# Moving the stack transfers of an attention-plus-GLU kernel into one unit, and shifting its score ring by 64 bytes

## The chip, the core and the metric

The kernel runs on one core of a Trainium2 chip. A core has TensorE (PE, matmuls; its weight loads are listed as PEld), VectorE (DVE), ScalarE (ACT), GpSimd (POOL) and SyncE (SP), which here issues nearly all DMA transfers. They work on SBUF, a memory of 128 partitions; matmuls write to PSUM. The metric is the device time of one execution in microseconds, the median over several runs; lower is better.

## The reference

The input x has 2048 rows (tokens) of 512 features. Two branches are mixed by a gate:

```
g = sigmoid(sum(x * gate_w))                     # one number per row
a = attention(x): qkv = x @ wqkv, 32 heads of 16 features,
    query i sees keys i-255 .. i (a sliding window of 256),
    softmax(q k^T / 4) v, then @ wo
b = (sigmoid(x @ w_gate) * (x @ w_up)) @ w_down  # 1376 inner features
out = g * a + (1 - g) * b
```

All of it is float32. The kernel keeps that accuracy by splitting a number into a high and a low part and adding three matmuls (high by high, high by low, low by high).

## The kernel before

**Tiles.** The rows are cut into 16 blocks of 128 (NB) and 4 chunks of 512 (NC), the heads into 8 groups of 4 (NG). One *unit* is one block of one head group; 128 units, numbered u, make the attention part, and the loop over u from L839 on writes down the work of all engines in the order in which they run it. A *score matmul* is one of the four per unit that `s_part` makes (L370, queries by keys, to find each row's maximum) or that `st_part` makes (L425, keys by queries, whose exponentials become the softmax weights). `st_part` runs 9 units behind `s_part` (LAG).

**Half-array matmuls.** A score matmul contracts 64 rows, half of TensorE. `s_part` and `st_part` take opposite halves, so one matmul of each goes through side by side. Between them stand the matmuls of the projections (`pj`) and of the GLU branch (`gu`), L282, which are split into two halves of 64 rows in the same manner. In every unit a pair of score matmuls is followed by two or three such pairs. Every 8 units, at u = 17, 25, 33, and so on, stands a burst of `pv` matmuls (L460, weights by values).

**The score ring.** The operands of the score matmuls lie in `ring`, three places of 16 KB per partition, each holding one *stack*: the queries and keys of 8 units (1024 columns), with extra rows for the low parts, for constants and for the row maxima. A stack is made thus: the projection is split into `sh` (high) and `sl` (low), both are stored to DRAM (`stack_scratch<-sh`, `stack_scratch<-sl`, 512 KB each), and they are read back in rows of another order by `stack_load`: one fill of constants (two for the first use of a place), one transfer of 512 KB and four of 256 KB, all into `ring`. The list is put into `sdma` at u = 9 for stack 2, and at u = 18, 26, 34, ... for the stacks 3 to 15. `transfers()` then issues at most SD = 3 of them in each unit (a module constant on L44), in the order in which SP reaches them, and with them what else is due: stores of finished `gu` tiles (`gu_scratch<-sp`), loads of the next GLU weights (`guraw`).

**The maxima.** A group of four units gives a table of row maxima. It is split on VectorE (`max_split`), stored to DRAM (`max_scratch<-nt`, L394, 16 KB) and read back into `ring` by two transfers of 8 KB (`max_load`, L401). The `st_part` matmuls of those rows need it, through the 128-byte pieces that it puts into the ring. From u = 13 on SP issues the store and the load in every fourth unit (13, 17, 21, ...), for the group that began five units earlier. The first two groups have their stores at u = 4 and 8 and their loads at u = 5 and 9, where the load stands behind `transfers()`.

**The issue order.** SP takes its transfers one after another, each with its waits, so a transfer that waits holds up all that stand behind it. All of them share 16 DMA engines.

**Addresses.** SBUF tiles are placed in the order in which they are declared. Before the change `ring` starts at byte 2176 of each partition, which is 128 modulo 256; x (`xh`, `xl`) and all weights of L282 start at 192 modulo 256. In the last part, the down projection (`pd`), `hb` are the stationary operands, at 128 modulo 256, and `ring` holds the moving ones.

Of the kernel before, what the change touches and what calls it, by code (L numbers as in the profile page):

```python
# [7 lines left out]
F32 = mybir.dt.float32  # L8
# [6 lines left out]
P = 128  # L15
# [9 lines left out]
NB = T // P  # L25
# [15 lines left out]
PVLAG = LAG + 4  # L41
WIDE = 2 * 4
NWIDE = NG - 1
SD = 3  # L44
QB = 32
HOLD = 3
GAPS = [3] * 12 + [2] * 3
# [18 lines left out]
def gated_mix_kernel(  # L66
# [40 lines left out]

    cpool = ctx.enter_context(tc.tile_pool(name="cpool", bufs=1))
    ps = ctx.enter_context(tc.tile_pool(name="ps", bufs=1, space=PSUM))
    ring_t = cpool.tile([P, 4, RING * CH2], F32R, name="ring")  # L110
    ring = [ring_t[:, :, r * CH2:(r + 1) * CH2] for r in range(RING)]
    gsum = cpool.tile([P, NB], F32, name="gsum")


    def ring_f(f):
# [28 lines left out]
    with ExitStack() as actx:  # L144
# [197 lines left out]
        def run_dmas(dmas):  # L342
            for dst, src in dmas:
                nc.sync.dma_start(dst, src)
# [494 lines left out]
        for u in range(N):  # L839
# [19 lines left out]
            def transfers():  # L859
# [5 lines left out]
                later.clear()  # L865
                run_dmas(sdma[:SD])
                del sdma[:SD]

# [116 lines left out]
            if u == N - 1:  # L985
                pctx.close()
                lpool = actx.enter_context(tc.tile_pool(name="lpool", bufs=1))
                gates = lpool.tile([P, 4 * NB], F32, name="gates")
                gs, omg = gates[:, 0:NB], gates[:, NB:2 * NB]
                spare = [lpool.tile([P, CH], F32, name=f"spare{k}") for k in range(6)]  # L990
            if u >= N - 2:
# [168 lines left out]
```

## Time and profile before

| | |
|---|---|
| three runs | 724.72, 722.93, 725.45 us; median 724.72 us |
| the profiled execution | 723.27 us |
| its span, first to last instruction | 721.4 us |
| TensorE busy | 713.5 us (99% of the span) |
| VectorE, ScalarE, GpSimd busy | 478.5, 430.4, 165.6 us |
| the 16 DMA engines, mean busy share over the span | 56.2% for SP's queue |
| granted TensorE clock, mean | 1.000 |

The profile gives for each group of instructions its line, engine, operands, count, busy time, mean length and the idle time before it with what ended that. A wait of TensorE can be seen twice: on PE (the matmul) and on PEld (the weight load that runs ahead of it). Matmuls are pipelined, so a matmul's length (0.39 us for 512 columns) is more than the distance from one start to the next on the same rows of the array; that distance is what a matmul costs.

### The profile page before, as it was taken

What the parts mean: (1) busy time and instruction counts of PE and PEld (TensorE: products, weight loads), DVE (VectorE), ACT (ScalarE), POOL (GpSimd) and SP (SyncE); (2) the same over time, 40 slices, a digit from 0 to 9 for tenths busy, and PEclk for the clock granted to TensorE, in tenths of its full rate; (3) what the DMA queues carried; (4) which work ended last, traced back from release to release, by engine and by line L of the source; (5) the groups of instructions that cost most, each with busy time, mean ns of one, the idle gap of its engine ahead of it and who ended that gap; (6) DMA issues with size and microseconds to landing.
All of it is one profiled execution on the core that took longest, in us unless ns stands there. A gap on an engine that the chain in (4) does not pass through costs nothing.

```text
span 721.4 us, 17549 instructions
## 1 busy us (share of the span) xinstructions
PE 713.5 (99%) x6298; PEld 606.1 (84%) x6298; DVE 478.5 (66%) x1455; ACT 430.4 (60%) x890; POOL 165.6 (23%) x254
## 2 busy tenths in 40 slices
PE   9999999999999999999999999999999999999997
PEld 7888889888798798988979889798788888888886
DVE  5369767657676676765667667676837767667481
ACT  6423766667676677766767667675676655435341
POOL 5200423223233233323324223232331000000000
PEclk9999999999999999999999999999999999999999
DMA  8465534646355364554645437465478978778531
GB/s 304 112 201 195 202 123 177 189 137 212 127 195 189 121 211 146 178 165 146 203 149 197 152 99 245 151 219 148 154 216 227 263 201 215 199 169 250 144 65 58
DMA packets 104814, 127.22 MB, mean 176 GB/s; under 512 B 46718, under 2 KB 63614, under 8 KB 104728
## 3 DMA queue, kind: packets, MB, share of 16 engines
q1 hardware_dynamic: 104584, 125.98, 56.2%
q8 instruction: 49, 0.80, 0.5%
q14 instruction: 37, 0.30, 0.1%
q10 hardware_dynamic: 144, 0.13, 0.1%
HBM read 71.80 MB, written 51.13 MB: 170 GB/s over the span
## 4 chain that ended last, share of the span: by engine, by line
PE 98%; DMA 1%; issue 0%; DVE 0%; DVEq 0%
PE gu L282 28%; PE pj L282 12%; PE pv L460 11%; PE s L370 6%; PE st L425 6%; PE tp L598 6%; PE pd L96 5%; PE pd L95 5%; PE pd L94 5%; PE vh L635 3%; PE pa L94 2%; PE pa L95 2%; PE pa L96 2%; PE vps L497 2%; DMA ring<-max_scratch 1%; PE pd L1088 1%
## 5 line engine op out<-in xcount | busy, mean ns | idle before, releaser
L376 DVE CUSTOM_DVE_ANT_0 junk<-s,mask 128x384 f32<-128x384 f32 (+2 forms) x512 | 271.9, 531 | 136.8 <-PE s L370 76.4
L282 PE MATMUL gu<-xh,w 64*128 64x512 f32 x1152 | 273.5, 392 | 0.0
L282 PE MATMUL gu<-xl,w 64*128 64x512 f32 x576 | 185.9, 389 | 0.0
L430 ACT ACTIVATE pbuf<-st 128x384 f32<-128x384 f32 (+2 forms) x288 | 138.3, 490 | 60.7 <-PE st L425 31.3
L425 PE MATMUL st<-ring 64*128 64x384 f32 (+2 forms) x536 | 166.6, 327 | 2.7 <-DMA ring<-max_scratch 2.5
L370 PE MATMUL s<-ring 64*128 64x384 f32 (+2 forms) x536 | 162.9, 322 | 0.0
L282 PEld LDWEIGHTS gu<-xh,w 64*128 64x128 f32 x1152 | 157.0, 185 | 5.3
L430 ACT ACTIVATE V<-st 128x384 f32<-128x384 f32 (+2 forms) x224 | 100.6, 454 | 51.9 <-PE s L370 24.9
L370 PEld LDWEIGHTS s<-ring 64*128 64x128 f32 x536 | 95.2, 184 | 14.1 <-issue 3.0
L436 POOL TENSOR_SCALAR_AFFINE_SELECT pbuf<-pbuf 128x512 f32<-128x512 f32 x72 | 46.8, 651 | 253.2 <-ACT pbuf L430 239.1
L425 PEld LDWEIGHTS st<-ring 64*128 64x128 f32 x536 | 95.9, 184 | 7.7 <-DMA ring<-max_scratch 1.9
L282 PEld LDWEIGHTS gu<-xl,w 64*128 64x128 f32 x576 | 92.0, 185 | 1.6
L282 PE MATMUL pj<-xl,wqh 64*128 64x512 f32 (+1 forms) x228 | 79.9, 389 | 0.0
L282 PE MATMUL pj<-xh,wqh 64*128 64x512 f32 (+1 forms) x228 | 79.8, 389 | 0.0
L282 PE MATMUL pj<-xh,wql 64*128 64x512 f32 (+1 forms) x228 | 69.8, 389 | 0.0
L95 PE MATMUL pd<-ring,hb 128*128 128x512 f32 x160 | 62.3, 390 | 0.0
L94 PE MATMUL pd<-ring,hb 128*128 128x512 f32 x160 | 62.3, 390 | 0.0
L96 PE MATMUL pd<-ring,hb 128*128 128x512 f32 x160 | 62.3, 390 | 0.0
L436 POOL TENSOR_SCALAR_AFFINE_SELECT V<-V 128x512 f32<-128x512 f32 x56 | 35.8, 640 | 111.2 <-ACT V L430 107.1
L90 ACT CAST hb<-V 128x512 fp32r<-128x512 f32 x40 | 24.9, 622 | 58.8 <-DVE V L798 44.2
L460 PE MATMUL pv<-pbuf,V 128*32 128x384 f32 (+2 forms) x848 | 49.5, 382 | 0.0
L442 POOL TENSOR_SCALAR_AFFINE_SELECT pbuf<-pbuf 128x512 f32<-128x512 f32 x70 | 44.9, 641 | 0.0
(131 smaller groups left out, 1243.4 us busy)
## 6 DMA issues: line engine op xcount, KB each, us to landing
gu_scratch<-sp SPq DMA_DIRECT2D x72, 256.0 KB
V<-gu_scratch SPq DMA_DIRECT2D x36, 512.0 KB
ring<-stack_scratch SPq DMA_DIRECT2D x56, 256.0 KB
stack_scratch<-sh SPq DMA_DIRECT2D x14, 512.0 KB
stack_scratch<-sl SPq DMA_DIRECT2D x14, 512.0 KB
ring<-stack_scratch SPq DMA_DIRECT2D x14, 512.0 KB
guraw<-in_wgu_dram SPq DMA_DIRECT2D x18, 256.0 KB
v_scratch<-V SPq DMA_DIRECT2D x4, 1088.0 KB
```

The costliest lines, as they stand in the source:

```text
L94: mm(ps, lh, rh, start=first, stop=False)
L95: mm(ps, lh, rl, start=False, stop=False)
L96: mm(ps, ll, rh, start=False, stop=last)
L282: return mm(pt, (wl if w == 2 else wh)[r, d], (xl if w == 1 else xh)[r, d, c * CH:(c + 1) * CH], start=k == 0 and not second, stop=k == 3 ...
L370: mm(pt[:, (k - k0) * P:(e - k0) * P], lhsT, blk(g, k, hh, 1, e - k), start=k == k0, stop=e == i + 1, skip_group_check=True,)
L376: nc.vector.tensor_tensor_reduce(junk[:, 0:n], pt[:, 0:n], mask[:, 3 * P - n:], scale=1.0, scalar=NEG, op0=ALU.add, op1=ALU.max, accum_out ...
L425: mm(pt[:, (q - j) * P:(e - j) * P], lhsT, blk(g, q, hh, 0, e - q), start=q == j, stop=e == last, skip_group_check=True,)
L430: exps.append(nc.scalar.activation(p_blk(u, hh, 0, n), pt[:, 0:n * P].rearrange("p (b t) -> p b t", t=P), AF.Exp, scale=SCALE,))
L436: nc.gpsimd.affine_select(buf[:, s0], buf[:, s0], pattern=[[0, HG], [1, P]], compare_op=ALU.is_ge, fill=0.0, base=0, channel_multiplier=-1,)
L442: nc.gpsimd.affine_select(old, old, pattern=[[0, HG], [-1, P]], compare_op=ALU.is_gt, fill=0.0, base=0, channel_multiplier=1,)
L460: mm(bank[32 * hh:32 * hh + w, (q - q0) * P:(e - q0) * P], vt[:, v:v + w], p_blk(g * NB + j, hh, q - j, e - q), start=j == j0, stop=j == q ...
L598: return mm(tp[b][:, 0:TW], (xl if w == 1 else xh)[r, d, b * P:(b + 1) * P], tw[d][int(w == 2)][r, 0:TW], start=k == 0 and not second, sto ...
```

## The change

Two things are changed.

First, SD goes from 3 to 7, so that all transfers of a stack are issued in the unit in which the list is made: u = 9 for stack 2 and u = 18, 26, ... for the others, each one unit behind a `pv` burst. Only SP's order changes; the rows of all other engines are the same. In 11 of the 14 stacks another row stood between the loads and no longer does.

Second, `gsum` (64 bytes per partition) is declared ahead of `ring` and no longer behind it. `ring` moves from byte 2176 to byte 2240, that is to 192 modulo 256, where x and the weights are. `gates` grows by 64 bytes so that `spare` and `hb`, declared behind it, move by the same amount and `hb` also stands at 192. All else stays where it was.

```diff
-SD = 3
+SD = 7
...
+    gsum = cpool.tile([P, NB], F32, name="gsum")
     ring_t = cpool.tile([P, 4, RING * CH2], F32R, name="ring")
     ring = [ring_t[:, :, r * CH2:(r + 1) * CH2] for r in range(RING)]
-    gsum = cpool.tile([P, NB], F32, name="gsum")
...
-                gates = lpool.tile([P, 4 * NB], F32, name="gates")
+                gates = lpool.tile([P, 5 * NB], F32, name="gates")
```

SP's rows at stack 2 (units 9 and 10). `ring<-stack_scratch` are the stack's loads, `ring<-max_scratch` is the load of the second table of maxima, `v_scratch<-V` a store of values of 1088 KB:

```order
 L344 DMA ring<-fill_scratch 4x2x1024 x2
 L344 DMA ring<-stack_scratch 32x4x1024
+L344 DMA ring<-stack_scratch 32x2x1024 x4
 L401 DMA ring<-max_scratch 4x16x32 x2
 L157 DMA v_scratch<-V 128x8x272
-L344 DMA ring<-stack_scratch 32x2x1024 x4
 L533 DMA guraw_0_1101<-in_wgu_dram 128x512
```

Four loads of 256 KB now stand ahead of the load of the maxima and of the store of the values.

SP's rows at stack 4 (units 26 to 29), with two stores of `gu` tiles and the store and load of a table of maxima at the end:

```order
 L344 DMA ring<-fill_scratch 4x2x1024
 L344 DMA ring<-stack_scratch 32x4x1024
-L344 DMA ring<-stack_scratch 32x2x1024
+L344 DMA ring<-stack_scratch 32x2x1024 x4
-L344 DMA gu_scratch<-sp_1_0_2008 128x512
-L344 DMA gu_scratch<-sp_2_0_2037 128x512
-L344 DMA ring<-stack_scratch 32x2x1024 x3
+L344 DMA gu_scratch<-sp_1_0_2011 128x512
+L344 DMA gu_scratch<-sp_2_0_2040 128x512
 L394 DMA max_scratch<-nt_2162 128x32
 L401 DMA ring<-max_scratch 4x16x32 x2
```

Three loads have moved past the two stores; the store of the maxima stands behind the same transfers as before.

## The prediction

> **What bounds the kernel now.** I read the page first: the span, TensorE's share, the chain of work that ended last, the costliest groups. Times are us.
>
> ```profile
> span 721.4 us, 17549 instructions
> PE 713.5 (99%) x6298; PEld 606.1 (84%) x6298; DVE 478.5 (66%) x1455; ACT 430.4 (60%) x890; POOL 165.6 (23%) x254
> ...
> PE 98%; DMA 1%; issue 0%; DVE 0%; DVEq 0%
> ...
> L370 PE MATMUL s<-ring 64*128 64x384 f32 (+2 forms) x536 | 162.9, 322 | 0.0
> ```
>
> TensorE sets the end, and the change neither adds nor removes a matmul. So only two things can move the time: the waits of TensorE, and the distance between neighbouring matmuls. The list of waits comes next; these are the rows of L425, on which a transfer can act.
>
> ```profile
> PEld st L425 <- DMA ring<-max_scratch: 1.9, 2, 1.1
> PEld st L425 <- issue: 1.7, 1, 1.7
> PEld st L425 <- ACT V L430: 0.9, 2, 0.5
> ```
>
> Five weight loads of L425 wait 1.9 + 1.7 + 0.9 = 4.5 in all (0.6%). The timeline puts them in units 31, 47, 79, 95 and 111, the last units of a head group but one each time a new stack's maxima are first read. I followed one through SP's timeline, the windows (engine columns, then granted clock, DMA busy share, GB/s) and the chain.
>
> ```profile
> 137.28 1.27 SPq L344 DMA_DIRECT2D ring<-stack_scratch  x2
> 138.66 0.99 SPq L344 DMA_DIRECT2D gu_scratch<-sp  x2
> 139.71 2.05 SPq L344 DMA_DIRECT2D ring<-stack_scratch  x3
> 142.41 0.33 SPq L394 DMA_DIRECT2D max_scratch<-nt  x1
> 147.64 1.16 SPq L401 DMA_DIRECT2D ring<-max_scratch  x2
> ```
> ```profile
> 139.00:140.00 1.00, 1.00 (x12) 0.99 (x10) 0.86 (x4) 0.52 (x2) 0.72 (x2) 1.00 0.76 131
> 140.00:141.00 1.00, 1.00 (x13) 1.00 (x11) 0.86 (x3) 0.61 (x2) 0.50 (x1) 1.00 0.93 188
> 141.00:146.00 5.00, 5.00 (x50) 5.00 (x48) 3.86 (x17) 3.73 (x9) 1.22 (x2) 1.00 0.96 355
> 146.00:147.50 1.50, 1.50 (x18) 1.50 (x16) 0.91 (x5) 1.50 (x5) 1.23 (x2) 1.00 0.12 36
> ```
> ```profile
> 147.64 1.86 DMA ring<-max_scratch
> ```
>
> The store of the maxima, 16 KB, is issued at 142.41 behind some 2 MB. The DMA engines are full until about 146.1, SP gets the store's completion at 147.64, and the load takes 1.86 more: TensorE goes on at 149.5. So the wait hangs on when the transfers ahead of the store are through. In VectorE lies no help: the store's issue at 142.41 is its own.
>
> **The change, part by part.**
>
> *Eleven reordered stacks.* What is ahead of the store of the maxima is the same before and after; three loads only go ahead of two stores. A full set of DMA engines gains nothing from another order. It gains only where they were not full: 0.24 in 139 to 140 and 0.07 in 140 to 141, together 0.31, since the loads at 139.71 stood behind a store that waited for ScalarE. But loads issued one behind the other don't fill the engines from the start either; stacks with that order are in the trace already, one of them here:
>
> ```profile
> 439.71 3.19 SPq L344 DMA_DIRECT2D ring<-stack_scratch  x5
> ...
> 446.82 0.32 SPq L394 DMA_DIRECT2D max_scratch<-nt  x1
> 451.41 1.19 SPq L401 DMA_DIRECT2D ring<-max_scratch  x2
> ```
>
> This stack has all five loads in one run, and it precedes the longest wait of the five, 1.7. So I take half of 0.31 for each of the four other waits: -0.6. Ends: 0, and -2.8 (4.5 less 1.7: all four waits gone). On SP the loads take 2.05 for three, so the two `gu` stores are issued 2.05 later; the buffers they free (tag `sp`, five of them) come round only after five further copies, several units later, which hides it. If that cover were gone, ScalarE's copies out of PSUM would be late next, and then the matmuls that refill it.
>
> *Stack 2, in units 9 and 10.* Here the four loads of 256 KB go ahead of the load of the second table of maxima and of a store of 1088 KB.
>
> ```profile
> 67.65 1.98 SPq L344 DMA_DIRECT2D ring<-fill_scratch  x2
> 69.73 0.64 SPq L344 DMA_DIRECT2D ring<-stack_scratch  x1
> 70.49 1.12 SPq L401 DMA_DIRECT2D ring<-max_scratch  x2
> 71.66 0.46 SPq L157 DMA_DIRECT2D v_scratch<-V  x1
> 72.17 4.61 SPq L344 DMA_DIRECT2D ring<-stack_scratch  x4
> ```
> ```profile
> 75.95 0.34 PE L425 MATMUL st<-ring 64*128 64x384 f32 x1
> ```
>
> That L425 at 75.95 is the first of `st_part`(2), in unit 11, whose columns reach into the second group of maxima: it needs the load now issued at 70.49. How long do the five loads take alone? Two rows of a stack whose loads stand together:
>
> ```profile
> 257.99 3.19 SPq L344 DMA_DIRECT2D ring<-stack_scratch  x5
> ```
> ```profile
> 264.00:265.00 1.00, 1.00 (x13) 1.00 (x11) 0.68 (x4) 0.85 (x2) 0.99 (x2) 1.00 0.17 61
> ```
>
> From 257.99 to 264.2 (a share of 0.17 in the last us) are 6.2. From 69.73 that is 75.9; the maxima's pieces stand behind, and completion is seen 1.5 later (146.1 to 147.64 above), 77.4, or 1.86 later, 77.8. Against 75.95 the matmul is 1.5 to 1.8 late: +1.6, new. Ends: 0, if the small pieces slip through between the loads, and +3, if the loads go as slowly as the four above (4.61 to issue, against four fifths of 3.19). The store of 1088 KB is not needed before its read-back at 86.42, 10 us later; the bytes up to there are the same.
>
> *The ring's address.* A weight load runs beside the matmul ahead of it on the same rows. Neighbours of one kind (L282 and L282) read both at 192 modulo 256, a score matmul and an L282 one at 128 and 192, and after the change at 192 and 192. No row shows that pair with equal addresses; the nearest are the starts of one stretch, one half of the array:
>
> ```profile
> 253.41 0.39 PE L282 MATMUL pj<-xh,wql 64*128 64x512 f32 x1
> 253.65 0.39 PE L282 MATMUL pj<-xh,wql 64*128 64x512 f32 x1
> 253.88 0.39 PE L282 MATMUL pj<-xh,wql 64*128 64x512 f32 x1
> 254.11 0.34 PE L370 MATMUL s<-ring 64*128 64x384 f32 x1
> 254.28 0.39 PE L282 MATMUL gu<-xh,w 64*128 64x512 f32 x1
> ```
> ```profile
> 528.48 0.36 PE L598 MATMUL tp<-tail_hb,xl 64*128 64x450 f32 x1
> 528.68 0.36 PE L598 MATMUL tp<-tail_hb,xh 64*128 64x450 f32 x1
> 528.88 0.34 PE L425 MATMUL st<-ring 64*128 64x384 f32 x2
> 529.06 0.36 PE L598 MATMUL tp<-tail_wqh,xh 64*128 64x450 f32 x1
> ```
> ```profile
> 35.36 2.72 PE pj L282 x12
> ```
>
> L282 to L282, equal: 0.24 and 0.23. L282 to score, unequal: 0.23. Score to L282: 0.17 for 384 columns. The whole array, equal: 2.72 / 12 = 0.2267 for 512, or 0.170 for 384. Later, 450 columns take 0.20 both before an equal neighbour (528.48 to 528.68) and before a score matmul (528.68 to 528.88). So I take 0: the row that differs in the address alone shows no difference. Upper end: the step before a score matmul rises from 0.23 to the 0.235 that equal neighbours take in this stretch, 0.005 times 536: +2.7. Lower end: the step of a score matmul, 0.17 and 0.18 (528.88 to 529.06), falls from its mean, 0.175, to 0.170: -0.005 times 536, -2.7.
>
> The Trainium skill, page "SBUF — State Buffer", section "Who interferes with whom", says that TensorE has one read port for the moving operand and an independent one for weight loads, and that it never waits on anyone. By it the shift is worth nothing and the sum stays; the steps of 0.24 and 0.23 for the same work show that something small varies that it doesn't name.
>
> `gates`, `spare` and `hb` move together with the ring, so a `pd` matmul's two operands stay equal to each other: 0, as does the work of VectorE and ScalarE on them beside a TensorE that is 99% busy.
>
> **Sum.** -0.6 + 1.6 + 0 = +1.0. On the profiled execution, 723.27 (its span and 1.9 around it), 724.3; it lies 1.45 under the median of the runs, 724.72, so against the median 725.7. Within 0.3%, 2.2 us, about what a measurement of this kernel can tell from no change.
>
> **Rivals.**
>
> *Equal addresses cost.* For it: L282 beside L282, equal, has the slowest steps. Against: the 450-column rows. Place: all units. 725.7 + 2.7 = 728.4, slower; it decides where the step before a score matmul grows by over 0.0022 (the 1.2 that the sum leaves up to 2.2, over 536).
>
> *The order helps.* The four waits go and the new one at unit 11 doesn't come: 724.72 - 2.8 = 721.9, faster. For it: none of the four is over 1.1, and the store of the maxima needs to be through only that much sooner. Against: the stack at 439.71.
>
> *Equal addresses help*, by the lower end: 725.7 - 2.7 = 723.0. For it: 0.17 to 0.18 against 0.170. Against: nothing in the rows of equal neighbours is that fast on half the array.
>
> *The change doesn't do what it says.* Three stacks had their loads together already, and if the maxima slip through at unit 11, nothing moves: 724.7.
>
> **How the numbers follow.** The sum: 0.36 (within 0.3% 0.19; slower 0.17, with the upper end at unit 11). Equal addresses cost: 0.22, slower. The order helps: 0.21 (faster 0.18, within 0.03). Equal addresses help: 0.15 (faster 0.08, with some of the waits gone too; within 0.07). Nothing moves: 0.06 (within 0.05, slower 0.01). Faster 0.26, same 0.34, slower 0.40. The range: from 719.5, where the order and the addresses both help (721.9 - 2.7 = 719.2), to 730, the first rival's 728.4 with the upper end at unit 11 (1.4 more, 729.8). The sum's own range is 724.1 to 727.1, the ends of unit 11.
>
> **What would show it.** The profile after should have a wait of L425 for `ring<-max_scratch` near 76, of 1.5 to 1.8; five loads in one run in SP's timeline at 136 to 141, and the load of the maxima issued 0.1 to 0.3 sooner after the store than 5.2; the wait at unit 111 as it was; and the steps before and after score matmuls as quoted. The prediction is wrong if those steps change by 0.005 or more, if the wait at 76 is absent, or if a wait appears that the list doesn't have now, on ScalarE's copies for instance.

## The result and the profile after

The changed kernel takes 730.38 us (median of 7 runs, 728.46 to 732.65), the kernel before 724.72 on the same chip: ratio 1.0079, 95% interval 1.0056 to 1.0101: slower, by an interval that lies above 1. The forecast was 725.7, with a range up to 730.0. The profiled execution took 729.14, its span is 727.1, 5.7 more than before.

The page after, its span, busy times and chain:

```profile
span 727.1 us, 17546 instructions
PE 716.7 (99%) x6298; PEld 604.0 (83%) x6298; DVE 478.6 (66%) x1455; ACT 431.0 (59%) x890; POOL 166.2 (23%) x254
...
PE 97%; DMA 2%; SPq 0%; issue 0%; ACT 0%; DVE 0%; DVEq 0%
```

TensorE's busy time grew by 3.2 with the same 6298 matmuls; the rest of the 5.7 is time in which it stood. The list of waits, rows of L425:

```profile
PE st L425 <- DMA ring<-max_scratch: 4.5, 4, 1.5
PEld st L425 <- issue: 3.2, 2, 1.9
PEld st L425 <- DMA ring<-max_scratch: 2.7, 2, 1.8
PEld st L425 <- ACT V L430: 1.7, 2, 1.4
PE st L425 <- ACT V L430: 1.0, 1, 1.0
```

There are more of them than before, and one kind is new: L425 waits on PE itself for ScalarE's `V<-st`. To see where, the start of each unit (its first `s_part` matmul) in the two traces is set side by side. The lead of the kernel before grows so:

| stretch | grows by, us |
|---|---|
| up to the start of unit 0 (initial loads) | 0.7 |
| unit 11 | 1.9 |
| units 12 to 111, evenly, 0.02 per unit | 1.9 |
| the five waits of before (units 31, 47, 79, 95, 111), net | -0.1 |
| unit 117 | 1.4 |
| from unit 118 to the end | -0.1 |

**Unit 11** is the wait that the prediction had. SP's timeline after, TensorE's row, and the chain:

```profile
70.40 3.76 SPq L344 DMA_DIRECT2D ring<-stack_scratch  x5
74.21 1.34 SPq L401 DMA_DIRECT2D ring<-max_scratch  x2
75.65 0.40 SPq L157 DMA_DIRECT2D v_scratch<-V  x1
```
```profile
78.50 0.41 PE L425 MATMUL st<-ring 64*128 64x384 f32 x1 [1.52 <-DMA ring<-max_scratch]
```
```profile
74.21 4.15 DMA ring<-max_scratch
```

All five loads of stack 2 go ahead, the two small loads of maxima land 4.15 after their issue, and the matmul that stood at 75.95 starts at 78.50. The table gives the loss, 1.9, since the start of the program also lies 0.7 later.

**Unit 117** is a wait that the prediction didn't have. Stack 15 is loaded in unit 114, where a load of GLU tail weights (`tailraw`, L575, 225 KB) also stands in SP's queue. Before, it went out after two loads of the stack; after, behind all five. SP's timelines before and after:

```profile
471.07 1.26 SPq L344 DMA_DIRECT2D ring<-stack_scratch  x2
472.38 0.58 SPq L575 DMA_DIRECT2D tailraw<-in_wgu_tail_dram  x1
...
473.48 1.89 SPq L344 DMA_DIRECT2D ring<-stack_scratch  x3
```
```profile
475.53 3.19 SPq L344 DMA_DIRECT2D ring<-stack_scratch  x5
478.76 0.58 SPq L575 DMA_DIRECT2D tailraw<-in_wgu_tail_dram  x1
```

The chain after goes through it; then ScalarE's and TensorE's rows after, and ScalarE's before:

```profile
478.76 5.47 DMA tailraw<-in_wgu_tail_dram
484.25 0.57 ACT tail_hb L588
484.82 0.40 ACT V L430
```
```profile
484.25 0.57 ACT L588 CAST tail_hb<-tailraw 128x450 fp32r<-128x450 f32 x1 [1.90 <-DMA tailraw<-in_wgu_tail_dram]
...
485.26 0.44 PE L425 MATMUL st<-ring 64*128 64x384 f32 x1 [0.97 <-ACT V L430]
```
```profile
477.87 0.56 ACT L588 CAST tail_hb<-tailraw 128x450 fp32r<-128x450 f32 x1
```

The load takes 5.47. ScalarE, which works in order, stands 1.90 at the split of these weights; the exponentials behind it are late, the PSUM tiles they read don't come free, and TensorE waits for them. Before, the same split had no wait.

**The drift** has no wait at all. Between units 49 and 78 neither kernel waits; the first matmuls of the two units, before and after:

```profile
220.45 0.38 PE L370 MATMUL s<-ring 64*128 64x256 f32 x1
...
327.44 0.33 PE L370 MATMUL s<-ring 64*128 64x384 f32 x1
```
```profile
223.45 0.38 PE L370 MATMUL s<-ring 64*128 64x256 f32 x1
...
331.07 0.33 PE L370 MATMUL s<-ring 64*128 64x384 f32 x1
```

29 units take 106.99 before and 107.62 after, 0.022 more for each unit.

### The profile page after: what moved, and what is told of

The parts are those of the page before. It is cut to its first block, busy times and chain, and to the rows that moved or that the text cites. A ratio compares the mean times of both kernels' runs of the same rounds, so it can differ in the third digit from the quotient of the medians.

```text
span 727.1 us, 17546 instructions
## 1 busy us (share of the span) xinstructions
PE 716.7 (99%) x6298; PEld 604.0 (83%) x6298; DVE 478.6 (66%) x1455; ACT 431.0 (59%) x890; POOL 166.2 (23%) x254
## 4 chain that ended last, share of the span: by engine, by line
PE 97%; DMA 2%; SPq 0%; issue 0%; ACT 0%; DVE 0%; DVEq 0%
PE gu L282 27%; PE pj L282 12%; PE pv L460 11%; PE st L425 6%; PE s L370 6%; PE tp L598 6%; PE pd L94 5%; PE pd L95 5%; PE pd L96 5%; PE vh L635 3%; PE pa L94 2%; PE pa L95 2%; PE pa L96 2%; PE vps L497 2%; DMA ring<-max_scratch 1%; DMA tailraw<-in_wgu_tail_dram 1%
## 5 line engine op out<-in xcount | busy, mean ns | idle before, releaser
L282 PE MATMUL gu<-xh,w 64*128 64x512 f32 x1152 | 275.0, 394 | 0.0
L282 PE MATMUL gu<-xl,w 64*128 64x512 f32 x576 | 186.2, 391 | 0.0
L425 PE MATMUL st<-ring 64*128 64x384 f32 (+2 forms) x536 | 165.4, 325 | 5.4 <-DMA ring<-max_scratch 4.5
L282 PEld LDWEIGHTS gu<-xh,w 64*128 64x128 f32 x1152 | 155.3, 184 | 8.4
L425 PEld LDWEIGHTS st<-ring 64*128 64x128 f32 x536 | 95.7, 184 | 11.7 <-issue 3.2
L282 PEld LDWEIGHTS gu<-xl,w 64*128 64x128 f32 x576 | 91.1, 184 | 2.0
L282 PE MATMUL pj<-xh,wqh 64*128 64x512 f32 (+1 forms) x228 | 80.4, 392 | 0.0
L282 PE MATMUL pj<-xl,wqh 64*128 64x512 f32 (+1 forms) x228 | 80.3, 391 | 0.0
L282 PE MATMUL pj<-xh,wql 64*128 64x512 f32 (+1 forms) x228 | 70.3, 391 | 0.0
```

Of the source, the lines that this page charges most:

```text
L282: return mm(pt, (wl if w == 2 else wh)[r, d], (xl if w == 1 else xh)[r, d, c * CH:(c + 1) * CH], start=k == 0 and not second, stop=k == 3 ...
L425: mm(pt[:, (q - j) * P:(e - j) * P], lhsT, blk(g, q, hh, 0, e - q), start=q == j, stop=e == last, skip_group_check=True,)
```

## The experiments

Theory A: these are three separate costs, two waits of small loads behind a stack, and the address; the order of the steady stacks costs and gains nothing. Rivals: all of the loss is the order (B), all of it is the address (C), the drift comes from the transfers (D). All kernels compute the whole reference.

### Each part alone

The order alone:

```diff
-SD = 3
+SD = 7
```

> SD = 7 alone, the ring at its old address. Theory A (three separate costs: 1.9 us in unit 11 for the maxima behind stack 2, 1.4 us in unit 117 for a GLU weight load behind stack 15, about 0.02 us per unit from the ring's address): 1.9 + 1.4 = 3.3 us over the kernel before, ratio 1.0046, both waits there, and units 12 to 116 as long as before. Rival B (all of the loss is the order): 5.7 us over, 1.008. Rival C (all of it is the address, the waits are only where TensorE stands anyway): 0, ratio 1.000.

727.92 us, ratio 1.0040 (1.0022 to 1.0057). B's 1.008 and C's 1.000 both lie outside. There is no drift: units 49 to 78 take 107.01. The wait in unit 11 is there, 2.1, that in unit 117 costs 0.95. But unit 11 lost 3.5 in this execution, and the windows say why (engine columns, then granted clock, DMA share, GB/s):

```profile
76.00:79.00 3.00, 1.27 (x12) 0.83 (x10) 1.13 (x4) 0.49 (x1) 1.22 (x2) 0.97 1.03 371
79.00:83.00 4.00, 4.00 (x26) 4.00 (x25) 2.09 (x6) 2.39 (x6) 0.00 (x0) 0.60 0.57 192
83.00:90.00 7.00, 7.00 (x69) 7.00 (x67) 4.98 (x21) 5.15 (x12) 2.44 (x4) 1.00 0.12 40
```

After the wait the clock is down to 0.60 over 4 us; with the 0.97 ahead of it that is 0.40 x 4 + 0.03 x 3 = 1.7 of lost clock. (In this profile the same happened once more after unit 111.) The last section comes back to it.

The address alone:

```diff
-    ring_t = cpool.tile(...)        # and after it gsum
+    gsum = cpool.tile([P, NB], F32, name="gsum")
+    ring_t = cpool.tile(...)
...
-                gates = lpool.tile([P, 4 * NB], F32, name="gates")
+                gates = lpool.tile([P, 5 * NB], F32, name="gates")
```

> The new address alone, SD = 3. Theory A: neither of the two waits; the starts of the units fall behind those of the kernel before by 0.02 us in each unit, 2.1 us in all from unit 12 on, ratio 1.003. Rival B (order): 0. Rival C (address): 5.7 us, 1.008. Rival D (the drift comes from transfers and not from the address, by way of the memory that they share with TensorE): 0, and the drift is in the run with SD = 7 alone.

725.26 us, ratio 1.0016 (0.9999 to 1.0034): C's 1.008 is out, and A's 1.003 is inside. The runs alone don't tell it from no change; the trace does. Neither of the two waits is there, and the drift is:

```profile
220.76 0.38 PE L370 MATMUL s<-ring 64*128 64x256 f32 x1
...
328.33 0.34 PE L370 MATMUL s<-ring 64*128 64x384 f32 x1
```

107.57 against 106.99. So the drift comes with the address and not with the order, and D falls.

The two parts alone add up to 1.0056, the changed kernel stands at 1.0079. The difference, about 1.7 us, is no more than the three intervals allow, and no run shows what it is.

### The steady stacks, and the two stacks taken out

The order of the eleven stacks between, at the old address:

```diff
-SD = 3
+SD = 7
...
-                run_dmas(sdma[:SD])
-                del sdma[:SD]
+                n = 3 if u < LAG + 3 or u in (114, 115, 116) else SD
+                run_dmas(sdma[:n])
+                del sdma[:n]
```

> The old address; SD = 7 except for stacks 2 and 15, so only the steady stacks in between are issued in one run. Theory A: 0 within 0.3 us in the profile (1.000 within what the runs tell), the waits in units 31, 47, 79, 95 and 111 stay about 4.5 us in all. What the prediction took: 0.6 us under the kernel before, 0.9992. Rival D (drift from transfers): 2.1 us over, spread over all units.

724.31 us, ratio 1.0000 (0.9982 to 1.0018). In the profile its last unit starts 0.28 sooner than before, 0.09 of which lies ahead of unit 0. The reordered stacks are worth nothing that can be told from zero.

The changed kernel with the same edit, stacks 2 and 15 in threes again, the new address kept:

> The changed kernel, but stack 2 and stack 15 keep three transfers per unit (units 9 to 11, 114 to 116). Theory A: 3.3 us under the changed kernel, 2.1 to 2.4 over the kernel before (1.003), no wait of TensorE in units 11 and 117, the drift left. Rival B: as before, 1.000. Rival C: as the changed kernel, 1.008.

725.47 us, ratio 1.0021 (1.0005 to 1.0037), 4.9 under the changed kernel's median, where 3.3 was expected. No wait in units 11 and 117; units 49 to 78 take 107.59. What is left is the address. A part of the surplus may be lost clock: three of the changed kernel's seven runs have a mean granted clock of 0.997 or 0.998, and they are its three longest (731.08, 731.70, 732.65). That they lost it after unit 11 is not shown, for only one of the seven was profiled.

### The small loads ahead of the stack

Here the stacks stay in one unit and the small loads are moved ahead:

```diff
-            if not mark:
-                transfers()
             if u in (5, LAG):
                 max_load(u // 4 - 1)
+            if not mark:
+                transfers()
...
-TAIL_LOAD = {109: 0, 110: 1, 114: 2, 115: 3}
+TAIL_LOAD = {109: 0, 110: 1, 112: 2, 113: 3}
```

> The changed kernel with its stacks in one unit and its address, but the second load of maxima is issued ahead of stack 2 (unit 9), and the last two loads of GLU tail weights in units 112 and 113, ahead of stack 15. If the two waits are those of small loads behind the stack: both go with the stacks left as they are, 3.3 us under the changed kernel, 1.002 to 1.003 of the kernel before. If they come from the 1.25 MB of a stack in one run as such (TensorE waits for the stack or for buffers): they stay, 1.008.

726.51 us, ratio 1.0018 (0.9999 to 1.0036), 3.9 under the changed kernel's median. SP's timeline, then TensorE's and ScalarE's rows:

```profile
68.53 1.87 SPq L401 DMA_DIRECT2D ring<-max_scratch  x2
...
71.60 3.22 SPq L344 DMA_DIRECT2D ring<-stack_scratch  x5
```
```profile
76.69 0.33 PE L425 MATMUL st<-ring 64*128 64x384 f32 x1
```
```profile
484.45 0.56 ACT L588 CAST tail_hb<-tailraw 128x450 fp32r<-128x450 f32 x1
```

Neither place has a wait any more, with five loads of each stack in one run as in the changed kernel. So what cost was not the run of loads but who stood behind it.

But the second move made a new wait, in unit 115, where TensorE starts 1.3 late. SP's wait for VectorE, its rows, and TensorE's:

```profile
SPq L575 <- DVE tail_wql L590: 6.8, 1, 6.8
```
```profile
470.37 0.42 SPq L394 DMA_DIRECT2D max_scratch<-nt  x1
...
475.20 1.13 SPq L401 DMA_DIRECT2D ring<-max_scratch  x2
```
```profile
477.22 0.41 PE L425 MATMUL st<-ring 64*128 64x384 f32 x1 [0.90 <-DMA ring<-max_scratch]
```

The tail load that now stands in unit 112 has to wait 6.8 for its buffer, until VectorE has split an earlier one, and the store of the maxima stands behind it: it goes out at 470.37, in the changed kernel at 464.28. This execution is the longest of the twelve (729.82); whether the others have that wait is not on record.

### The address

Seven layouts more, all with SD = 3. Two of them as diffs: the ring at its new place with x and the weights moved on as well (so that they differ by 64 bytes as before), and a ring 128 bytes below x.

```diff
+    gsum = cpool.tile([P, NB], F32, name="gsum")
     ring_t = cpool.tile(...)
-    gsum = cpool.tile([P, NB], F32, name="gsum")
+    pad = cpool.tile([P, NB], F32, name="pad")
```

> SD = 3; the ring at 192 modulo 256 as in the changed kernel, but x and the weights moved on by 64 bytes too, to 0, so that the two differ by 64 bytes as in the kernel before; hb at 192 with the ring. If the drift hangs on the difference between the two addresses: none, the time of the kernel before (1.000), units 33 to 78 as long as before. If it hangs on where the ring itself stands: 0.02 us per unit, 2.0 us over, ratio 1.003, as with the new address alone.

```diff
     ring_t = cpool.tile(...)
+    pad = cpool.tile([P, NB], F32, name="pad")
     gsum = cpool.tile([P, NB], F32, name="gsum")
...
-                gates = lpool.tile([P, 4 * NB], F32, name="gates")
+                gates = lpool.tile([P, 3 * NB], F32, name="gates")
```

> SD = 3; the ring at 128 modulo 256 as before, x and the weights at 0, so that they differ by 128 bytes; hb at 128. If only equal addresses cost: no drift, 1.000. If the cost falls with the distance: less than none, units 33 to 78 shorter than before by up to 0.02 us each, 2 us under in all, 0.997. If it is neither, the size of the drift says so.

The ring 64 above x (a pad of 128 bytes in the same place; 64 bytes taken off a scratch tile of VectorE to make room):

> SD = 3; the ring at 128 modulo 256, x and the weights at 64, so that the ring stands 64 bytes above x and no longer 64 below; hb at 128. If what counts is the distance modulo 128 (64 good, 0 and 128 bad): no drift, 1.000 of the kernel before. If only the distance of the kernel before is good: 0.02 us per unit, 1.003.

Pads of 32 bytes, with `gsum` ahead of the ring and behind it:

> SD = 3; the ring 32 bytes below x and the weights (192 and 224 modulo 256), hb at 192. With 64 below there is no drift, with 0 there is 0.02 us per unit. If the cost changes evenly with the distance: half of it, 1 us, 1.0015. If 64 below is a single good place: 2 us, 1.003.

> SD = 3; the ring 96 bytes below x and the weights (128 and 224 modulo 256), hb at 128. With 64 below there is no drift, with 128 there is 0.024 us per unit. If the cost changes evenly with the distance: half of it, 1.2 us, 1.0015. If 64 below is a single good place: 2 us, 1.003.

And two in which the weights of L282 leave the residue of x, as the ring does. Below x (`wq_pool` and `w0` are declared ahead of `xh`, `gsum` between, `gates` 3 * NB), and above (a pad between `xl` and `w0`):

> SD = 3; the weights of the projections and of the GLU branch stand where the ring does, at 128 modulo 256, and x alone at 192, so that every weight load of an L282 matmul is 64 bytes below the x that streams beside it, as the ring's already is; hb goes to 64, 64 bytes below the ring that streams beside it in the down projection. If a distance of 64 bytes is what makes a step short whoever reads: the steps between two L282 matmuls fall from about 18.3 ns over their columns to about 15, some 3.4 ns for each of 1360 steps, 4.6 us, 0.994, and the down projection gets shorter too. If the distance counts only around score matmuls: 1.000. If the steps only pass the loss on to one another: units 33 to 78 as long as before within 0.2 us.

> SD = 3; as the run with the weights 64 bytes below x, but 64 bytes above it (weights at 0, x at 192, ring at 128; hb at 192, 64 above the ring). If only the distance modulo 128 counts: as that run between two L282 matmuls, 0.994 to 0.997, but ring and weights are 128 apart where a score matmul streams. If the sign counts: 1.000 or above.

Distances in bytes modulo 256; the stretch is from the first score matmul of unit 49 to that of unit 78, in which TensorE has no wait that it doesn't have before:

| ring to x | weights to x | units 49 to 78, us | per unit over before | ratio (95% interval) |
|---|---|---|---|---|
| -64 (before) | 0 | 106.99 | | |
| -64 (both moved) | 0 | 107.08 | 0.003 | 1.0004 (0.9984 to 1.0024) |
| -32 | 0 | 107.25 | 0.009 | 0.9994 (0.9973 to 1.0015) |
| 0 (address alone) | 0 | 107.57 | 0.020 | 1.0016 (0.9999 to 1.0034) |
| +64 | 0 | 107.58 | 0.020 | 1.0024 (1.0003 to 1.0044) |
| 128 | 0 | 107.71 | 0.025 | 1.0005 (0.9986 to 1.0023) |
| -96 | 0 | 108.16 | 0.040 | 1.0029 (1.0008 to 1.0051) |
| -64 | -64 | 107.63 | 0.022 | 1.0051 (1.0027 to 1.0076) |
| -64 | +64 | 108.14 | 0.040 | 1.0083 (1.0052 to 1.0113) |

Four kernels with the layout of before and another order of transfers take 107.01 to 107.08, and three with the distance 0 take 107.57 to 107.62, so 0.1 is what this stretch mostly varies by. There are exceptions: the kernel with the small loads ahead, also with the distance 0, takes 107.97, 0.4 of it in units 63 and 64 alone, and of the 0.26 at 32 below, 0.18 lies in unit 64 alone. Without that one unit, 32 below is as good as before. The rows of the layout moved as a whole, and of the one with 96 bytes:

```profile
220.21 0.38 PE L371 MATMUL s<-ring 64*128 64x256 f32 x1
...
327.29 0.33 PE L371 MATMUL s<-ring 64*128 64x384 f32 x1
```
```profile
224.48 0.38 PE L371 MATMUL s<-ring 64*128 64x256 f32 x1
...
332.63 0.34 PE L371 MATMUL s<-ring 64*128 64x384 f32 x1
```

The layout moved as a whole is as good as before: it is the distance that counts, not the place. But of the rules that were tried none holds. Equal addresses are not what costs: 64 above, 128 and 96 below cost as much or more. It is not the distance modulo 128, for 64 above is bad. It is not an even slope around 64 below, for 32 below is as good and 96 below is the worst. And moving the weights to 64 below x made it worse, where it had been hoped to make the steps shorter; but in the last two rows the distance from the ring to the weights changes as well, to 0 and to 128, so they don't tell the one pair from the other. The runs at 128 and at 96 below come out closer to before than their drift in the profile (0.025 x 100 = 2.5, 0.040 x 100 = 4.0) would have it: their intervals stop short of it, at 1.0023 and 1.0051. Why one distance is cheaper than another stays open.

Taken from the starts of all neighbouring pairs on the two halves (means, 512 columns, a score step 384): the step before a score matmul grows from 228.2 to 233.1 ns with the change, the score step itself shrinks from 176.0 to 173.7, the step after it grows from 232.3 to 235.5, and steps among L282 go from 231.8 to 231.2. The three around a score matmul sum to +5.8 ns; with four such pairs per unit that is 0.023, the drift. The step after the score matmul has an L282 stream and an L282 weight load beside it, whose addresses the change leaves alone, and yet it grew: by these means the effect is not one of a pair alone.

### The five old waits

If the 16 KB store of the maxima is late because of the bytes ahead of it, taking bytes away must help. First three of a stack's loads were held back until the maxima were through:

```diff
-                run_dmas(sdma[:SD])
-                del sdma[:SD]
+                if u % 16 not in (11, 12) or u < 26:
+                    run_dmas(sdma[:SD])
+                    del sdma[:SD]
```

> The kernel before, but of the stacks whose loads begin at u = 26, 42, 58, ... the last three 256 KB loads are issued behind the load of the maxima at u = 29, 45, 61, ... and not in the units before it. If the waits in units 31, 47, 79, 95 and 111 are those of a 16 KB store behind the transfers ahead of it: all five go, 4.5 us, ratio 0.994. If the bytes ahead don't matter: 1.000 with the waits there. If the stack is then late for its first score matmuls in units 32, 48, ...: new waits there, 1.000 or above.

725.85 us, ratio 1.0002 (0.9981 to 1.0023). The five waits went, and others came: the score matmul waits for its own stack in unit 32, it stands again at the start of unit 64 (the profile names VectorE there, which had been through for 0.5 us), and the `pv` burst of u = 113 waits for values whose load stood behind the held ones.

```profile
153.16 0.29 PE L370 MATMUL s<-ring 64*128 64x128 f32 x1 [0.38 <-DMA ring<-stack_scratch]
```
```profile
458.80 0.53 PE L460 MATMUL pv<-pbuf,V 128*32 128x384 f32 x4 [1.54 <-DMA V<-v_scratch]
```

So the third outcome: a wait exchanged for a wait. What can be held without anyone waiting soon are the stores of GLU tiles:

```diff
+            hold = u > 26 and u % 16 in (11, 12, 13) and u < NU
             def transfers():
                 if mark and visits.get(u) != 2:
-                    run_dmas(later[:2])
-                    del later[:2]
+                    if not hold:
+                        run_dmas(later[:2])
+                        del later[:2]
                     max_load((u - 5) // 4)
-                run_dmas(later)
-                later.clear()
+                if not hold or mark:
+                    run_dmas(later)
+                    later.clear()
...
-                    run_dmas(later)
-                    later.clear()
+                    if not hold:
+                        run_dmas(later)
+                        later.clear()
                     max_store((u - 5) // 4)
```

> The kernel before, but the stores of GLU tiles that fall due in units 27 to 29, 43 to 45, ... are issued behind the load of the maxima in units 29, 45, ... and the stack's loads stay ahead. 512 KB less are ahead of the 16 KB store, about 1.5 us of full DMA engines. If the waits in units 31, 47, 79, 95 and 111 hang on the bytes ahead of the store: the four under 1.1 us go, 111 falls to 0.2 or less, 4 us in all, 0.9945, and the loads of values and of the stack are not late, as they were when the stack's loads were held. If the five buffers of the stores run out: ScalarE's copies late, waits of TensorE for them, 1.000 or above.

720.56 us, ratio 0.9931 (0.9906 to 0.9957): faster, and the five waits are gone but for 0.2. SP's timeline and the windows at the place that the prediction looked at:

```profile
137.17 3.20 SPq L344 DMA_DIRECT2D ring<-stack_scratch  x5
142.44 0.32 SPq L394 DMA_DIRECT2D max_scratch<-nt  x1
145.56 1.18 SPq L401 DMA_DIRECT2D ring<-max_scratch  x2
146.83 1.38 SPq L344 DMA_DIRECT2D gu_scratch<-sp  x3
```
```profile
141.00:144.00 3.00, 3.00 (x31) 3.00 (x30) 2.41 (x12) 2.05 (x5) 1.22 (x2) 1.00 0.99 380
144.00:146.00 2.00, 2.00 (x21) 2.00 (x20) 1.41 (x5) 1.66 (x4) 0.00 (x1) 1.00 0.14 43
```

The DMA engines are through at about 144.3 (0.14 of the next 2 us), where before they were full until 146.1; the load of the maxima goes out 3.12 after the store's issue and no longer 5.2. But in unit 126 a new stand came:

```profile
510.22 0.44 PE L370 MATMUL s<-ring 64*128 64x384 f32 x1 [1.34 <-DVE mx L376]
```

There no stack is loaded and stores were held for nothing. With the bound moved:

```diff
-            hold = u > 26 and u % 16 in (11, 12, 13) and u < NU
+            hold = u > 26 and u % 16 in (11, 12, 13) and u < 112
```

> The kernel with the stores of GLU tiles behind the load of the maxima, but only up to unit 109: in units 123 to 125, where no stack is loaded, the stores go out as in the kernel before. In the run without this bound there was a stand of 1.5 us at the first matmuls of unit 126. If held stores had run out of buffers there: the stand goes, 1.4 us under that run, 0.991 of the kernel before, and the five waits stay away. If it was another cause: 0.993 as that run.

718.87 us, ratio 0.9923 (0.9904 to 0.9942), the fastest of all, 11.5 under the changed kernel's median. The stand in unit 126 is gone, so it came from holding stores there; whether by the buffers or by the queue was not told apart. One wait is new in this execution, again for values, at the burst of u = 113:

```profile
455.59 0.85 PE L460 MATMUL pv<-pbuf,V 128*32 128x384 f32 x8 [0.76 <-DMA V<-v_scratch]
```

## Why the prediction was wrong, step by step

*The eleven reordered stacks, -0.6.* The mechanism was off. The loads do go out in one run (in the profile after at 140.45), and the stores of GLU tiles 2 us later, without a wait of ScalarE for a buffer; but the load of the maxima is issued no sooner after the store:

```profile
140.45 3.19 SPq L344 DMA_DIRECT2D ring<-stack_scratch  x5
143.75 1.02 SPq L344 DMA_DIRECT2D gu_scratch<-sp  x2
145.22 0.32 SPq L394 DMA_DIRECT2D max_scratch<-nt  x1
150.58 1.19 SPq L401 DMA_DIRECT2D ring<-max_scratch  x2
```

It is 5.36 (145.22 to 150.58), against 5.23 before, where 4.9 to 5.1 was forecast. The five waits change by -0.1 net, the run of the eleven stacks alone has ratio 1.0000. The sentence "a full set of DMA engines gains nothing from another order" was right, and the 0.31 allowed beyond it is not there. That the wait hangs on the bytes ahead of the store was right as well: with 512 KB less ahead all five waits went.

*Stack 2, +1.6.* Right in place and mechanism, 1.9 in size: the maxima were forecast to be seen at 77.4 to 77.8, that is 78.1 to 78.5 with the later start, and the chain has them at 74.21 + 4.15 = 78.36. Its upper end, 3, left out that a wait of 2.1 can be followed by 1.7 of lost clock.

*The ring's address, 0.* This is one of the two steps that failed: the term was put at nothing. It measured 1.9 to 2.0, inside its ends (2.7), by the sign of the first rival; the step before a score matmul grew by 0.0049, over the 0.0022 from which that rival decided. The row on which the 0 rested, the two 450-column steps of 0.20, comes from 528 us, after the last unit (127 starts at 515.0). Units 122 to 126, in which such 450-column matmuls have taken the place of L282, show no drift after the change either; units 12 to 111 do. The row was taken from a stretch with other operands and other widths than the one that was to be priced. And the rival's reason, that equal addresses cost, isn't the cause, as the table shows.

By the Trainium skill, page "SBUF — State Buffer", section "Who interferes with whom", TensorE's two read ports are independent and it never waits on anyone, so the time should not hang on the layout. In these runs it does: 0.020 to 0.040 per unit between layouts that differ in hardly anything but the distance, with no new wait in the profile.

*The store of GLU tiles, `gates`, `hb`, VectorE, ScalarE: 0.* Right for the stores and for `hb` (from unit 118 to the end the difference does not grow).

*The other rivals.* That the order helps falls with the five waits, that equal addresses help with the drift, and that nothing happens with all three.

*What was left out* is the other step that failed: that a stack's loads go ahead in one run was followed past `gu` stores and maxima, but not past the `tailraw` load in unit 114. The text named a new wait on ScalarE's side as a thing that would make it wrong, and that is how it came, 1.4 in unit 117, by a load that ScalarE splits rather than by its buffers.

The terms as measured, 1.9 + 1.9 + 1.4 - 0.1 = 5.1, on the median of before give 729.8, against 730.38. The 0.7 ahead of unit 0 is none of the change's: unit 0 starts between 37.91 and 39.31 in the profiles of these kernels, at 38.63 with SD = 7 alone, whose program is that of before up to unit 9. The chances had given slower the largest share, 0.40, though the sum itself said within 0.3%.

## What to carry to other kernels

When transfers are bundled, list every transfer in that queue which they pass, at every place where the bundle occurs, and ask of each small load who waits for it, and of a load that is moved ahead whether its buffer is free by then; two of fourteen places made up the whole cost of the order. A late small store is helped by fewer bytes ahead of it, not by another order of the same bytes, and the bytes to move are those that nobody reads soon. A price for a layout has to come from rows of the stretch and of the operands that it is meant for; otherwise measure it, over a stretch without waits.

## What the runs showed of the hardware

**A wait can cost its length and then 1.7 us more.** In the profiles of all these kernels TensorE stood ten times for more than 2.0 us between units 11 and 112 (start to start on one half of the array, less the usual step of the matmul ahead). Seven of these stands (2.0 to 2.7) were followed by a granted clock of 0.50, and in each the clock lost in the windows sums to about 1.7 us, that is some 3.4 us at half speed; three (2.1, 2.4, 2.6) were not, nor was any of the shorter ones. The Trainium skill, page "TensorE: Matmul & The Clock Gate", Part 1, has the half rate and a window of about 3.4 us that runs on its own; the length agrees, but it asks for an idle window of that length, and here 2.0 us of standing sufficed.

**The waits seem to carry most of the scatter.** The five units 31, 47, 79, 95 and 111 took 21.0 to 25.0 us together in the profiles of the kernels in which nothing was held back, and 17.6 to 17.8 in the two with stores held. The runs of the kernel before scatter over 7.5 us (722.15 to 729.65, 23 runs), those of the fastest over 1.4 (718.30 to 719.71, 6 runs); 6 runs of the kernel with the weights 64 above, which has the waits, scatter over 4.6.

**Layouts act differently on whole-array matmuls.** In the down projection, where a weight load and the stream beside it use all rows, the mean step of 512 columns is 226.8 ns with equal addresses (before and after), 229.0 with the weights 64 bytes below, and 233.3 with them 64 above; from the start of unit 127 to the end the last of these takes 209.8 us where the kernel before takes 206.4.
